# A new hand-written order for the prologue of a block-sparse attention and gated MLP kernel

## The chip, the core and the metric

The kernel runs on one core of a Trainium2 chip. A core has a matrix engine (TensorE, PE in the profile) and three engines that work on whole tiles: VectorE (DVE), ScalarE (ACT) and GpSimd (POOL). SyncE (SP) only issues transfers here. Each engine executes its own queue of instructions in order, and waits on semaphores for what the others make. The metric is the device time of one execution in microseconds (us), and the time given is the median of several.

## The reference

There are 4 batches, 8 heads, 768 positions and 64 elements per head. Every query attends to the keys less than 16 positions away and to 24 summaries, one for each block of 32 positions (the maximum of the block's keys, and the mean of its values). The result goes through a gated MLP with 512 inputs, 1536 hidden columns and 512 outputs. The weights are float64, everything else is float32.

```python
k_sum = k.reshape(B, H, nb, block, D).max(axis=3)
v_sum = v.reshape(B, H, nb, block, D).mean(axis=3)
mask_l = np.abs(pos[:, None] - pos[None, :]) < window
scores_l = np.where(mask_l, scale * q @ k^T, -1e9)
scores_s = scale * q @ k_sum^T + np.log(block)
a = softmax(concat([scores_l, scores_s]))
x = a @ concat([v, v_sum])              # to [3072 tokens, 512]
g = x @ w_gate
out = (g * sigmoid(g) * (x @ w_val)) @ w_out
```

## The kernel before, in words

The 3072 tokens are worked off in six chunks `k` of 512. Attention of a chunk is done for four head pairs `u`, and the MLP of a chunk for twelve slices `j` of 128 hidden columns.

**Products.** Each MLP product is split into a high and a low part of both operands and needs three matmuls. `gate(k,j)` and `val(k,j)` (L654, tiles `g` and `v`) have 4 x 3 matmuls of 128x512, and so has `down(k,j)` (L701, tiles `acc`). With a third number, as in `gate(0,0,2)`, a step does only the three matmuls of one head pair. `silu` (ACT, L660) reads `g` and writes tile `a`, `mul` (DVE, L665) multiplies it by `v`, `ah` (ACT, L189) rounds it and `al` (L185) takes the rest. Two buffers of `a` exist, so `silu(0,j)` must wait until `al` of the slice before the last has read its `a`. `gate` and `val` share two banks of PSUM, so a `val` begins when the `silu` that reads the older bank is done.

**Weights.** A slice of the weights comes as raw float64 (`w_load`, L208, on SP) and is decoded on the chip: `w_abs` (ACT), four DVE steps `w_c1` L222, `w_c2` L226, `w_s1` L234 and `w_s2` L241, then `w_hi` (a rounding copy, L189 on ACT or L191 on DVE), and last `w_lo` (a subtraction with two inputs in SBUF, L185, on DVE as `=d` or on POOL as `=p`). A `gv` slice is 1024 wide and holds gate and value weights, an `o` slice 512 wide.

**Attention of one head pair.** `keys(1,u)` writes the pooled keys into the key windows `kw`: a POOL copy (L191) from `ks`, and where a batch begins also a DVE reduction (L343) that makes the new `ks` and a second POOL copy. There is one buffer of `ks` for each `u`, so the reduction must wait until the first copy has read the old one. Then come `scores` (PE, banks shared with `g`, `v` and `xo`), `ttr` (DVE, L512), `exp`, `rcp`, `nrm` (L555, on POOL, DVE or ACT), two transposes `tr` (PE, `pp`), their copies `pt`, `out` (PE, `xo`), `split` and `rest` (the high and low part of x, `xh` and `xl`). In chunk 0, `sw` and `sp` make the scores, and `out` and `outp` the products with values and pooled values. A number behind an engine letter in `sw`, `tr` or `fv` asks for so many filler matmuls of 128 columns on the zero tile `warm` (L747). They compute nothing.

**Order.** The first part of the program (all of chunk 0's MLP, the attention of chunks 0 and 1 and all weight decoding) is written as a string of 457 steps, `PROLOGUE`. Each step issues its instructions in turn, and a dependency ties every instruction to the one before it on its engine, so the string alone decides the order on each of the five queues:

```python
for name, args, on in read_steps(PROLOGUE):
    step[name](*args)
for x in traced[n_before:]:
    if x.engine in last:
        after(x, last[x.engine])
    last[x.engine] = x
```

The other five sixths of the MLP follow in a loop that the change doesn't touch.

Of the kernel before, what the change touches and what calls it, by code (L numbers as in the profile page):

```python
# [107 lines left out]
kf(2) qf(2) qf(0) sw(0,2)=cc pool(2) sp(0,2) kf(0) ttr0(0,2) pool(0) exp0(0,2) ttr1(0,2) exp1(0,2)
sw(0,0)=yg2 sp(0,0) kq(1) cst() kq(3) ttr0(0,0) pool(1) rcp(0,2) nrm(0,2)=p ttr1(0,0) exp0(0,0) w_load(0,g)
sw(0,1)=yg6 sp(0,1) w_load(1,gv) vr() ve() exp1(0,0) ttr0(0,1) vo() tr0(0,2)=c9 ttr1(0,1) rcp(0,0) w_abs(0,g)  # L110
exp1(0,1) w_c1(0,g) pool(3) exp0(0,1) w_c2(0,g) w_s1(0,g) w_abs(1,gv) rcp(0,1) tr1(0,2)=g sw(0,3)=cy4 sp(0,3)
ttr0(0,3) nrm(0,0)=p tr0(0,0)=c3 ttr1(0,3) exp0(0,3) exp1(0,3) pt0(0,2)=a w_s2(0,g) w_c1(1,gv) w_c2(1,gv)
rcp(0,3) tr1(0,0)=y nrm(0,1)=p tr0(0,1)=y6 w_s1(1,gv) tr1(0,1)=c nrm(0,3)=d w_s2(1,gv) fv()=g pt1(0,2)=a
w_load(0,v) out(0,2)=c pt0(0,0)=a fvc()=a outp(0,2) pt1(0,0)=a out(0,0)=c tr0(0,3)=c pt0(0,1)=a w_load(0,o)
w_abs(0,v) pt1(0,1)=a w_c1(0,v) w_hi(0,g)=a w_c2(0,v) w_abs(0,o) outp(0,0) tr1(0,3)=y w_lo(0,g)=d w_hi(1,gv)=a
w_s1(0,v) w_load(2,gv) w_c1(0,o) w_s2(0,v) w_load(3,gv) w_lo(1,gv)=d w_c2(0,o) out(0,1)=y split(0,0)=a rest(0,0)
w_s1(0,o) pt0(0,3)=a pt1(0,3)=a outp(0,1) w_abs(2,gv) split(0,1)=a w_load(1,o) w_hi(0,v)=a out(0,3)=g outp(0,3)
room(0) rest(0,1) gate(0,0,0) split(0,2)=a gate(0,0,1) rest(0,2) gate(0,0,2) split(0,3)=a rest(0,3) w_c1(2,gv)
w_abs(3,gv) gate(0,0,3) gate(0,1) silu(0,0) w_c1(3,gv) w_c2(2,gv) w_s2(0,o) w_lo(0,v)=p w_s1(2,gv) w_c2(3,gv)
w_s2(2,gv) w_abs(1,o) val(0,0,0) val(0,0,1) silu(0,1) w_hi(0,o)=a val(0,0,2) w_s1(3,gv) w_c1(1,o) val(0,0,3)  # L120
load(1,0) val(0,1) w_hi(2,gv)=a w_lo(2,gv)=d w_load(2,o) w_c2(1,o) mul(0,0) ah(0,0)=a keys(1,0) gate(0,2)
w_abs(2,o) mul(0,1) w_lo(0,o)=d w_s1(1,o) al(0,0)=d ah(0,1)=a w_s2(3,gv) w_load(3,o) w_load(4,gv) silu(0,2)
scores(1,0) down(0,0) val(0,2) w_s2(1,o) w_hi(3,gv)=a al(0,1)=d ttr0(1,0) pool_values(1,0) ttr1(1,0)
w_lo(3,gv)=p w_abs(4,gv) w_abs(3,o) w_c1(4,gv) w_c1(2,o) w_c2(4,gv) gate(0,3) mul(0,2) val(0,3) w_load(5,gv)
w_s1(4,gv) w_c1(3,o) w_s2(4,gv) exp1(1,0) w_hi(1,o)=a w_c2(3,o) w_lo(1,o)=d exp0(1,0) w_hi(4,gv)=a w_s1(3,o)
w_c2(2,o) w_s2(3,o) w_s1(2,o) w_load(7,gv) w_load(6,gv) rcp(1,0) down(0,1) w_lo(4,gv)=d load(1,1) silu(0,3)
w_abs(5,gv) w_hi(3,o)=a w_c1(5,gv) mul(0,3) gate(0,4) val(0,4) ah(0,2)=a w_abs(7,gv) w_c2(5,gv) w_lo(3,o)=d
w_s1(5,gv) w_s2(2,o) nrm(1,0)=a w_hi(2,o)=a w_s2(5,gv) al(0,2)=d w_hi(5,gv)=a tr0(1,0) silu(0,4) w_abs(6,gv)
w_load(4,o) tr1(1,0) pt0(1,0)=a w_abs(4,o) w_lo(2,o)=d pt1(1,0)=a down(0,2) keys(1,1) mul(0,4) w_c1(6,gv)
w_lo(5,gv)=d w_c1(4,o) scores(1,1) ah(0,4)=a w_c2(6,gv) ah(0,3)=a ttr0(1,1) exp0(1,1) ttr1(1,1) al(0,4)=d  # L130
w_load(5,o) load_values(1,0) w_load(7,o) w_load(6,o) w_c1(7,gv) w_s1(6,gv) values(1,0)=a w_load(9,gv) gate(0,5)
al(0,3)=p w_abs(5,o) w_c2(4,o) w_s2(6,gv) w_load(8,gv) w_s1(4,o) val(0,5) w_c2(7,gv) w_hi(6,gv)=a down(0,3)
# [5 lines left out]
w_c1(8,gv) w_lo(5,o)=d w_s2(9,gv) w_hi(9,gv)=a tr0(1,1) down(0,5) mul(0,7) ah(0,7)=a pt0(1,1)=a keys(1,2)
scores(1,2) pool_values(1,2) tr1(1,1) w_lo(9,gv)=d w_s2(6,o) w_abs(8,o) w_s1(7,o) gate(0,9) ttr0(1,2) ttr1(1,2)
pt1(1,1)=a w_c2(8,gv) out(1,1) ah(0,6)=a load(1,3) w_hi(6,o)=a w_lo(6,o)=d exp0(1,2) al(0,6)=p w_s2(7,o)  # L140
w_c1(8,o) exp1(1,2) w_hi(7,o)=a w_s1(8,gv) al(0,7)=d w_s2(8,gv) w_c2(8,o) val(0,9) down(0,6) w_lo(7,o)=d
w_abs(10,gv) w_abs(9,o) w_c1(9,o) w_hi(8,gv)=a w_c1(10,gv) w_lo(8,gv)=d down(0,7) silu(0,9) rcp(1,2) w_c2(10,gv)
w_s1(10,gv) mul(0,9) split(1,1)=a w_s2(10,gv) w_c2(9,o) nrm(1,2)=a gate(0,8) tr0(1,2) w_hi(10,gv)=a keys(1,3)
w_lo(10,gv)=d w_s1(8,o) val(0,8) ah(0,9)=a rest(1,1) room(1) w_load(11,v) w_load(11,g) silu(0,8) mul(0,8)
load_values(1,2) w_load(10,o) w_load(11,o) w_s2(8,o) pt0(1,2)=a al(0,9)=p w_abs(11,v) ah(0,8)=a w_hi(8,o)=a
w_s1(9,o) al(0,8)=d w_lo(8,o)=d gate(0,10) w_c1(11,v) tr1(1,2) pt1(1,2)=a w_c2(11,v) w_s2(9,o) w_s1(11,v)
w_s2(11,v) scores(1,3) ttr0(1,3) values(1,2)=a w_hi(9,o)=a silu(0,10) down(0,8) ttr1(1,3) val(0,10) w_abs(11,g)
w_c1(11,g) w_c2(11,g) w_lo(9,o)=p out(1,2) w_s1(11,g) w_s2(11,g) w_abs(10,o) exp1(1,3) w_hi(11,g)=d w_c1(10,o)
w_hi(11,v)=a down(0,9) w_lo(11,g)=p exp0(1,3) split(1,2)=d mul(0,10) w_lo(11,v)=d w_c2(10,o) rcp(1,3) ah(0,10)=a
rest(1,2) gate(0,11) w_abs(11,o) w_c1(11,o) w_c2(11,o) load_values(1,3) nrm(1,3)=a w_s1(10,o) tr0(1,3)  # L150
pt0(1,3)=a w_s2(10,o) al(0,10)=d w_hi(10,o)=a silu(0,11) pool_values(1,3) val(0,11) tr1(1,3) pt1(1,3)=a
values(1,3)=a w_s1(11,o) w_lo(10,o)=d down(0,10) w_s2(11,o) out(1,3) w_hi(11,o)=d w_lo(11,o)=p mul(0,11)
# [785 lines left out]
```

## Time and profile before

| | |
|---|---|
| time of the kernel, median of 3 runs | 674.9 us (674.82 to 676.22) |
| the profiled execution's own time | 675.49 us |
| its span in the profile | 673.7 us, granted clock 1.00 |
| PE busy | 667.8 us (99%) |
| DVE busy | 340.1 us (50%) |
| ACT busy | 297.4 us (44%) |
| POOL busy | 138.4 us (21%) |

The span is the time between the first and the last instruction of the profiled execution, and 1.8 us of that execution's time lie around it. A start in the trace counts from the start of the span. A duration on DVE or ACT includes an end that the next instruction overlaps: what an instruction costs in a queue that is full is the distance between two starts.

### The profile page before, as it was taken

The page shows a single profiled execution, that of the slowest core. Times are in us where ns is not written, and L with a number is a line of the kernel's source. Part 1 is how long each engine was busy: PE and PEld are TensorE (multiplying, and loading weights), DVE is VectorE, ACT ScalarE, POOL GpSimd, SP SyncE. Part 2 cuts the span into 40 slices and gives each one's busy share as a digit, 9 for nine tenths or more (in the row PEclk, how much of TensorE's full clock was granted, in tenths as well). Part 3 has the DMA queues.
Part 4 walks back from the last instruction along what each step waited for, and adds up shares of the span by engine and source line. Part 5 has one row for each costly group of instructions (what it writes and reads, how often), then busy time and mean ns, then how long its engine had stood idle before and what let it go on. Part 6 is the DMA issues. An engine that isn't in the chain of part 4 may idle for free.

```text
span 673.7 us, 12397 instructions
## 1 busy us (share of the span) xinstructions
PE 667.8 (99%) x4938; PEld 543.6 (81%) x4938; DVE 340.1 (50%) x952; ACT 297.4 (44%) x729; POOL 138.4 (21%) x131
## 2 busy tenths in 40 slices
...
GB/s 333 332 371 359 41 242 172 51 109 145 56 58 0 56 41 126 84 20 80 103 2 167 52 53 82 12 45 61 59 57 58 0 25 0 63 1 0 1 0 64
DMA packets 72059, 60.37 MB, mean 90 GB/s; under 512 B 42144, under 2 KB 60064, under 8 KB 70464
## 3 DMA queue, kind: packets, MB, share of 16 engines
...
## 4 chain that ended last, share of the span: by engine, by line
PE 97%; DVE 2%; DMA 1%; SPq 0%; issue 0%
PE g L654 30%; PE v L654 29%; PE acc L701 29%; PE xo L619 4%; PE sc L454 2%; DMA kq<-in_kF 1%; PE pp L570 1%; DVE p L512 1%; PE sc L465 1%; PE xo L627 1%; DVE ks L343 0%; PE pv L422 0%; PE end L701 0%; PE pp L747 0%; DVE m_g L226 0%
## 5 line engine op out<-in xcount | busy, mean ns | idle before, releaser
L701 PE MATMUL acc<-w_o,ah 128*128 128x512 f32 x572 | 176.2, 389 | 0.0
L654 PE MATMUL g<-xh,w_gv 128*128 128x512 f32 x480 | 159.7, 394 | 0.0
L654 PE MATMUL v<-xh,w_gv 128*128 128x512 f32 x480 | 157.9, 390 | 0.0
L665 DVE TENSOR_TENSOR a<-v,a 128x512 f32<-128x512 f32 x72 | 49.6, 689 | 199.8 <-PE v L654 198.1
L185 POOL TENSOR_TENSOR al<-a,ah 128x512 fp32r<-128x512 f32 x63 | 81.8, 1299 | 328.0 <-ACT ah L189 328.0
L701 PEld LDWEIGHTS acc<-w_o,ah 128*128 128x128 f32 x572 | 107.4, 188 | 22.2
L189 ACT CAST ah<-a 128x512 fp32r<-128x512 f32 x71 | 44.0, 621 | 168.5 <-DVE a L665 168.5
L701 PE MATMUL acc<-w_o,al 128*128 128x512 f32 x286 | 112.0, 392 | 0.0
L654 PEld LDWEIGHTS g<-xh,w_gv 128*128 128x128 f32 x480 | 90.1, 188 | 20.8 <-ACT w_o L189 0.2
L654 PEld LDWEIGHTS v<-xh,w_gv 128*128 128x128 f32 x480 | 90.1, 188 | 18.9
L660 ACT ACTIVATE a<-g 128x512 f32<-128x512 f32 x72 | 43.1, 599 | 134.7 <-PE g L654 131.7
L654 PE MATMUL g<-xl,w_gv 128*128 128x512 f32 x240 | 93.8, 391 | 0.0
L600 DVE STREAM_TRANSPOSE pt_short<-p_short 32x256 f32<-32x256 f32 x192 | 83.8, 436 | 19.8 <-POOL p_short L555 16.9
L654 PE MATMUL v<-xl,w_gv 128*128 128x512 f32 x240 | 93.4, 389 | 0.0
L701 PEld LDWEIGHTS acc<-w_o,al 128*128 128x128 f32 x286 | 53.7, 188 | 11.4 <-DVE al L185 0.2
L654 PEld LDWEIGHTS v<-xl,w_gv 128*128 128x128 f32 x240 | 45.1, 188 | 9.3
L654 PEld LDWEIGHTS g<-xl,w_gv 128*128 128x128 f32 x240 | 45.1, 188 | 8.8
L528 ACT ACTIVATE p_short<-p_short,nm 128x88 f32<-128x88 f32 x128 | 45.3, 356 | 0.2
L185 DVE TENSOR_TENSOR xl<-xo,xh 128x512 fp32r<-128x512 f32 x24 | 16.4, 686 | 57.0 <-ACT xh L189 56.9
L555 POOL TENSOR_TENSOR p_short<-p_short,ri 128x704 f32<-128x704 f32 x16 | 26.0, 1623 | 53.5 <-DVE ri L546 49.6
L654 PE MATMUL g<-xh,w_g 128*128 128x512 f32 x96 | 32.2, 396 | 0.0
L654 PE MATMUL v<-xh,w_v 128*128 128x512 f32 x96 | 31.6, 390 | 0.0
...
## 6 DMA issues: line engine op xcount, KB each, us to landing
raw_gv<-in_wgv SPq DMA_DIRECT2D x10, 1024.0 KB, 11.9
...
```

What stands on the lines that cost most here:

```text
L185: (nc.vector if e == "d" else nc.gpsimd).tensor_tensor(out=out, in0=a, in1=b.bitcast(F32), op=ALU.subtract)
L189: nc.scalar.copy(out, in_)
L454: nc.tensor.matmul(sc[h][s * SQ : (s + 1) * SQ, c * SC : (c + 1) * SC], t["q"][hs, i * SQ : (i + 1) * SQ], keys[hs], start=True, stop=True,)
L465: nc.tensor.matmul(sc[h][s * QT : (s + 1) * QT, c * KC : (c + 1) * KC], t["q"][hs, qs], t["kw"][hs, i, :], start=True, stop=True,)
L528: nc.scalar.activation(out=t["p"][:, i, :kc], in_=t["p"][:, i, :kc], func=AF.Exp, scale=-1.0, bias=t["nm"][:, i : i + 1], accum_out=t["sm" ...
L555: (nc.vector if on == "d" else nc.gpsimd).tensor_tensor(out=p, in0=p, in1=ri.rearrange("p (n o) -> p n o", o=1).broadcast_to([P, 2 * NTP, ...
L600: nc.vector.transpose(out=to[r * SQ : (r + 1) * SQ, :, s * SQ : (s + 1) * SQ], in_=t["p"][s * SQ : (s + 1) * SQ, :, at : at + SQ],)
L619: nc.tensor.matmul(ps[hs, qs], vw, t["pt"][:n, h, qs], start=k not in OWN or i == 0, stop=k not in OWN)
L654: nc.tensor.matmul(ps, w[:, cs], x, start=u == 0 and n == 0, stop=u == NP - 1 and n == 2)
L660: nc.scalar.activation(out=a, in_=A.pop(("g", k, j)), func=AF.Silu)
L665: nc.vector.tensor_tensor(out=a, in0=ps, in1=a, op=ALU.mult)
L701: nc.tensor.matmul(out, a[:, ts], w[:, cs], start=begin and n == 0, stop=end and n == 2)
```

## The change

The string is replaced by another order of the 457 steps. Some steps also get another engine: of the `w_lo`, 13 are on POOL instead of 6, five of them 1024 wide (slices 1, 3, 7, 9, 10) where there was one; of chunk 0's `al`, two are on POOL instead of four; `nrm(0,1)` goes from POOL to DVE. Chunk 0's first products are interleaved by head pair (`gate(0,0,0) gate(0,0,2) val(0,0,0) gate(0,0,1) ...`), with `w_v0` ready early, where all of gate slices 0 and 1 stood ahead of value slice 0. The fillers go from 37 units of 128 columns to 16 (of both, 7 are the opening ones). Two functions are adapted: slice 11's lead is on the other half, and `a_max` allocates its tiles in whichever half comes first. Line numbers from `a_max` on grow by one.

```diff
@@ PROLOGUE, the steps around keys(1,2), of 52 lines that are all new
-w_abs(7,o) w_abs(9,gv) w_c1(9,gv) w_c1(7,o) val(0,6) w_hi(7,gv)=a w_lo(7,gv)=d w_c2(9,gv) split(1,0)=a w_s2(5,o)
...
+rcp(1,1) silu(0,6) w_c1(6,o) w_c2(6,o) nrm(1,1)=a w_lo(7,gv)=p w_abs(8,gv) val(0,6) w_lo(4,o)=d keys(1,2)
...
     def w_lead(j, nm):
-        return LEAD if (nm, j) == ("v", NJ - 1) else 0
+        return LEAD if (nm, j) == ("g", NJ - 1) else 0
...
         t = U[k, u]
-        if g == 0 and k >= SHORT:
+        first = "p" not in t
+        if first and k >= SHORT:
             t["p"] = short["p"]
-        elif g == 0:
+        elif first:
...
-        if g == 0:
+        if first:
```

In the rows below a name is a tile with its slice or chunk and head pair, and a running number at its end; `w_gv7_1161<-m_gv7_1007` is a subtraction that makes the low half of weight slice 7.

POOL's queue from the first `w_lo` to the copies for the scores of chunk 1, head pair 2, before:

```order
L185 TENSOR_TENSOR w_v0_567<-m_v0_505,w_v0_567 128x512
L191 COPY kw_1_0_668<-ks_0_161 128x4x24
L191 COPY kw_1_0_668<-ks_0_696 128x4x24
L185 TENSOR_TENSOR w_gv3_776<-m_gv3_615,w_gv3_776 128x1024
L191 COPY kw_1_1_876<-ks_1_224 128x4x24
L191 COPY kw_1_1_876<-ks_1_973 128x4x24
L185 TENSOR_TENSOR al_0_3_1052<-a_0_3_881,ah_0_3_1001 128x512
L185 TENSOR_TENSOR w_o4_1128<-m_o4_956,w_o4_1128 128x512
L185 TENSOR_TENSOR al_0_5_1213<-a_0_5_1106,ah_0_5_1206 128x512
L191 COPY kw_1_2_1196<-ks_2_134 128x4x24
L191 COPY kw_1_2_1196<-ks_2_1286 128x4x24
```

The same stretch of POOL's queue, and one row more, of the change:

```order
L185 TENSOR_TENSOR w_gv1_568<-m_gv1_322,w_gv1_568 128x1024
L185 TENSOR_TENSOR w_o1_754<-m_o1_648,w_o1_754 128x512
L191 COPY kw_1_0_694<-ks_0_183 128x4x24
L191 COPY kw_1_0_694<-ks_0_775 128x4x24
L185 TENSOR_TENSOR w_gv3_835<-m_gv3_711,w_gv3_835 128x1024
L191 COPY kw_1_1_909<-ks_1_246 128x4x24
L191 COPY kw_1_1_909<-ks_1_1000 128x4x24
L185 TENSOR_TENSOR w_o2_1009<-m_o2_838,w_o2_1009 128x512
L185 TENSOR_TENSOR w_o3_1003<-m_o3_667,w_o3_1003 128x512
L185 TENSOR_TENSOR w_gv7_1161<-m_gv7_1007,w_gv7_1161 128x1024
L191 COPY kw_1_2_1054<-ks_2_134 128x4x24
L191 COPY kw_1_2_1054<-ks_2_1195 128x4x24
```

The subtractions of weight slices 1, 7 and 9 (the last in the next row) are now POOL's, `al_0_5` is no longer, and the copies of each head pair stand behind a subtraction of weights.

DVE's queue at the reduction for `keys(1,2)` before, where `ks_2_1286` is the new pooled keys:

```order
L185 TENSOR_TENSOR w_o5_1203<-m_o5_1054,w_o5_1203 128x512
L241 SCALAR_TENSOR_TENSOR m_gv9_1158<-raw_gv9_1037,m_gv9_1158 128x1024
L665 TENSOR_TENSOR a_0_7_1233<-v_0_7_1245,a_0_7_1233 128x512
L343 TENSOR_REDUCE ks_2_1286<-kt_1_2_1191 128x24
L363 TENSOR_REDUCE vr_1_2_1307<-vt_1_2_1199 128x24
L185 TENSOR_TENSOR w_gv9_1261<-m_gv9_1158,w_gv9_1261 128x1024
```

The same place in DVE's queue of the change:

```order
L185 TENSOR_TENSOR w_o4_1154<-m_o4_699,w_o4_1154 128x512
L343 TENSOR_REDUCE ks_2_1195<-kt_1_2_1049 128x24
L185 TENSOR_TENSOR xl_1_0_1127<-xo_1_0_1059,xh_1_0_1126 128x512
L666 TENSOR_TENSOR a_0_6_1165<-v_0_6_1180,a_0_6_1165 128x512
L234 SCALAR_TENSOR_TENSOR m_gv9_960<-raw_gv9_778,m_gv9_960 128x1024
L222 TENSOR_SCALAR m_o5_1093<-m_o5_1093 128x512
L226 TENSOR_SCALAR m_o5_1093<-m_o5_1093 128x512
L234 SCALAR_TENSOR_TENSOR m_o5_1093<-raw_o5_855,m_o5_1093 128x512
L234 SCALAR_TENSOR_TENSOR m_o6_1148<-raw_o6_1011,m_o6_1148 128x512
L241 SCALAR_TENSOR_TENSOR m_o5_1093<-raw_o5_855,m_o5_1093 128x512
L241 SCALAR_TENSOR_TENSOR m_gv9_960<-raw_gv9_778,m_gv9_960 128x1024
L185 TENSOR_TENSOR al_0_5_1253<-a_0_5_983,ah_0_5_1158 128x512
```

The reduction has moved ahead of `xl_1_0` and `mul(0,6)` (tile `a_0_6`), and `al_0_5` has come to DVE, eleven rows behind it.

## Rows read from the trace of the kernel before

**Rows 1.** The longest wait of PE behind the opening: us in total, times, longest.
```profile
PE sc L479 <- DMA kq<-in_kF: 0.9, 1, 0.9
```

**Rows 2.** Stretch, us, busy (count): PE, PEld, DVE, ACT, POOL; clock, DMA share, GB/s.
```profile
10.00:20.00 10.00, 9.66 (x159) 6.49 (x158) 9.86 (x58) 10.00 (x48) 5.44 (x3) 1.00 1.02 402
30.00:140.00 110.00, 110.00 (x718) 88.78 (x715) 108.12 (x221) 95.25 (x201) 18.91 (x20) 1.00 0.57 193
```

**Rows 3.** Timeline of PE up to the first gate product: start, duration, what.
```profile
1.46 3.35 PE L747 MATMUL warm<-warm 128*128 128x512 f32 x4 [1.46 <-DVE warm L809]
...
12.29 2.21 PE L747 MATMUL pp<-warm 128*128 128x512 f32 x6
...
23.68 1.15 PE L619 MATMUL xo<-pt,vrows 96*64 96x64 f32 x32
...
32.53 0.50 PE L654 MATMUL g<-xh,w_g 128*128 128x512 f32 x1
```

**Rows 4.** Timeline of SP: the last transfer that the `out` products need.
```profile
7.95 0.33 SPq L791 DMA_DIRECT2D vrows<-in_vO  x1
```

**Rows 5.** Transfers: queue, count, size, median us from issue to landing.
```profile
vrows<-in_vO SPq DMA_DIRECT2D x1, 1024.0 KB, 15.3
```

**Rows 6.** Timeline of POOL: start, duration, what, idle time before and its releaser.
```profile
14.61 1.85 POOL L555 TENSOR_TENSOR p<-p,ri 128x960 f32<-128x960 f32 x1 [0.88 <-DVE ri L546]
...
48.82 2.42 POOL L185 TENSOR_TENSOR w_gv<-m_gv,w_gv 128x1024 fp32r<-128x1024 f32 x1 [4.37 <-ACT w_gv L189]
...
91.23 1.29 POOL L185 TENSOR_TENSOR al<-a,ah 128x512 fp32r<-128x512 f32 x1 [8.53 <-ACT ah L189]
...
97.34 0.27 POOL L191 COPY kw<-ks 128x96 f32<-128x96 f32 x1 [4.41 <-DVE ks L343]
```

**Rows 7.** Timeline of DVE, 15 to 50 us.
```profile
15.59 1.15 DVE L226 TENSOR_SCALAR m_g<-m_g 128x512 int32<-128x512 int32 x1
...
22.96 1.15 DVE L555 TENSOR_TENSOR p<-p,ri 128x960 f32<-128x960 f32 x1
...
32.42 2.01 DVE L185 TENSOR_TENSOR xl<-xo,xh 128x512 fp32r<-128x512 f32 x3
...
37.90 0.68 DVE L226 TENSOR_SCALAR m_gv<-m_gv 128x1024 int32<-128x1024 int32 x1
38.50 1.22 DVE L241 SCALAR_TENSOR_TENSOR m_gv<-raw_gv,m_gv 128x1024 int32<-128x1024 int32 x1
...
42.24 0.42 DVE L226 TENSOR_SCALAR m_o<-m_o 128x512 int32<-128x512 int32 x1
42.57 0.68 DVE L665 TENSOR_TENSOR a<-v,a 128x512 f32<-128x512 f32 x1
43.17 0.94 DVE L343 TENSOR_REDUCE ks<-kt 128x24 f32<-128x768 f32 x1
44.03 0.68 DVE L665 TENSOR_TENSOR a<-v,a 128x512 f32<-128x512 f32 x1
```

**Rows 8.** Timeline of ACT, 28 to 41 us.
```profile
28.94 0.63 ACT L189 CAST xh<-xo 128x512 fp32r<-128x512 f32 x1
29.41 1.12 ACT L189 COPY pt<-pp 120x512 f32<-120x512 f32 x2
...
38.32 0.60 ACT L660 ACTIVATE a<-g 128x512 f32<-128x512 f32 x1 [1.20 <-PE g L654]
...
39.80 1.05 ACT L189 CAST w_gv<-m_gv 128x1024 fp32r<-128x1024 f32 x1 [0.37 <-DVE m_gv L241]
```

**Rows 9.** The chain that ended last, 88 to 106 us: start, length, what.
```profile
92.16 2.72 PE v L654 x12
94.89 0.44 PE pp L570 x4
...
98.07 0.98 PE sc L465 x32
...
102.39 1.08 PE xo L619 x32
```

More of the change, by code (lines that the diff above doesn't have):

```diff
@@ L107 @@
 PROLOGUE = """
[L108 to L132, printed above, removed]
@@ L138 @@
[L138 to L152, printed above, removed]
@@ new lines @@
+w_hi(0,g)=a w_s1(2,gv) split(0,0)=a w_hi(1,gv)=a outp(0,1) w_load(3,o) w_load(1,o) w_load(2,o) split(0,2)=a
+w_lo(0,g)=d split(0,1)=a outp(0,3) rest(0,0) rest(0,2) split(0,3)=a gate(0,0,0) rest(0,1) gate(0,0,2) rest(0,3)
+val(0,0,0) w_abs(0,o) w_c1(0,o) gate(0,0,1) w_abs(4,gv) gate(0,0,3) val(0,0,2) w_c2(0,o) silu(0,0) w_s1(0,o)
+w_c1(4,gv) w_load(5,gv) val(0,0,1) w_load(3,gv) room(0) w_s2(0,o) w_s2(2,gv) w_lo(1,gv)=p w_hi(2,gv)=a
+w_hi(0,o)=a val(0,0,3) w_abs(1,o) w_c2(4,gv) mul(0,0) gate(0,1) w_lo(2,gv)=d w_lo(0,o)=d w_abs(3,o) ah(0,0)=a
```

45 lines of the change are left out of this document (40 added, 5 removed).

## The prediction

> **What bounds the kernel now.** I first asked what the matrix engine waits for. The span holds two short stages. In the first, up to the first gate product at 32.53 us [rows 3], PE is not the limit. It has one wait of 0.9 us there [rows 1] and fills the other gaps with products on the zero tile (six of them, 2.21 us, at 12.29 [rows 3]). The transfers are the limit: between 10 and 20 us the DMA engines are fully busy at 402 GB/s [rows 2]. The last transfer that the `out` products need, `vO`, is issued at 7.95 [rows 4] and takes 15.3 us [rows 5], so it lands at 23.2. The first `out` starts at 23.68, and from there PE works without a gap to the gate at 32.53 (8.85 us) [rows 3].
>
> From the gate on PE itself is the limit. Between 30 and 140 us it is busy for 110.0 of 110 us, but DVE is close behind it with 108.1, while POOL has 18.9 [rows 2]. So PE's time is safe only as long as DVE's queue, or what DVE waits for, is not late. Here the reader should look: there is hardly any room on DVE, and any wait in its queue comes out on PE a little later.
>
> **The prices.** In a full DVE queue an instruction costs its duration less the 0.08 that the next one overlaps [rows 7]: two inputs of 1024 columns 1.14, two inputs of 512 columns 0.60, one input of 1024 columns 0.60, one input of 512 columns 0.34, the reduction 0.86; and 0.12 more for a decoding step with one input right behind the step that it reads (an estimate from the gaps of this kind). A subtraction of weights of 1024 columns costs POOL 2.42, one of 512 columns 1.29, a copy into `kw` 0.27 [rows 6]. On ACT, `silu` is 0.60 and a rounding copy of 1024 columns 1.05 [rows 8]. On PE a group of twelve matmuls is 2.72, scores 0.98, four transposes 0.44, `out` 1.08 [rows 9].
>
> **One price decides.** DVE and POOL hinder each other on SBUF. POOL's `nrm` runs from 14.61 to 16.46 [rows 6]. DVE's `w_c2` starts inside it at 15.59 and takes 1.15 [rows 7] where another of its size takes 0.42 [rows 7]: it ends 0.28 after POOL does. So I count a DVE instruction with two SBUF inputs, or one of the fast one-input ones, as held until POOL's subtraction ends, and POOL's likewise. The change puts seven more `w_lo` on POOL, at twice DVE's price (2.42 against 1.14).
>
> The Trainium skill (SBUF — State Buffer, "SBUF: two separate sides") says the same more strictly: the pair of ports that GpSimd and VectorE share is an exclusive lock, held for the whole instruction by whichever started first. The row of 1.15 agrees. By that rule, moving subtractions to POOL frees DVE of nothing while POOL's run overlaps such DVE work; its sum is the forecast's; by the opposite reading DVE would gain 1.14 for each, and the sum would be that of the second rival. The sum below goes by the rows alone.
>
> **Before the gate: nothing, at best.** `vO` stands behind the same bytes in both orders (`raw_v0` went ahead of it and `raw_g0` behind it, both 512 KB), so it lands at 23.2 again, and four `out`, four `outp` and two pairs of transposes still lie behind it. The fillers that go (21 units) lay in gaps that the transfers make, and leave idle time. On DVE the new order has `nrm(0,1)` more (1.07; POOL had it) before `nrm(0,3)`, which was at 22.96 [rows 7] and comes to about 24.1. Behind it stand two inputs of 1024, 960 and five of 512 columns with the one-input steps of `g0` and `gv2`: 1.07 + 1.14 + 0.46 + 0.46 + 0.72 + 0.60 + 0.72 + 0.72 + 1.14 = 7.0, so `w_lo(0,g)` starts at 31.1, and with its 0.60 and `xl_0_0`'s 0.68 x is ready at 32.4. PE arrives at 32.5. I take 0. From below the bound is -0.5 (23.68 less 23.2); the upper one is the first rival.
>
> **The scores of chunk 1, pair 0: +0.8.** The last `xl` ends at 34.4 now (32.42 + 2.01 [rows 7]) and at about 34.1 in the new order. From there DVE has 22 instructions to the end of `w_lo(4,gv)`: six of two inputs and 1024 columns (6.84), seven of two and 512 (4.20), five of one and 1024 (3.00), four of one and 512 (1.36), five pauses (0.60): 16.0, to 50.1. POOL's `w_lo(1,o)`, ready during the last, is held until its end: 1.29, then the copy 0.27, on which DVE's reduction waits (0.86), then the second copy 0.27, with 0.2 for four hand-overs: 2.9, so the scores can start at 53.0. PE has seven groups of 2.72 from 32.53, and about 0.6 for changes of tile: 52.2. In the old order there were five groups, and no wait.
>
> **The scores of pair 2: +3.3.** DVE stays full from 34.1 to `w_lo(4,o)`, 102 instructions: 15 of two inputs and 1024 columns (17.1), 24 of two and 512 (14.4), 12 of one and 1024 (7.2), 13 of one and 512 (4.4), four reductions (3.4), 16 steps of maxima at 0.20 (3.3) and two `rcp` (0.6), 50.4 in all; with the wait above (0.9) and pauses (1.3) it gets to 86.7. PE has 18 groups (49.0), two scores (2.0), two pairs of transposes (1.0), `out` (1.1), 0.8 of waiting and some 0.4 of changes, and begins `down(0,4)` at 86.8. So both arrive there together, and about then, at 86.6, POOL starts `w_lo(7,gv)`.
>
> Now the chain. POOL takes 2.42 and the copy 0.27: 89.3. DVE waits for that copy with its reduction (2.7 us idle, with `xl_1_0` and `mul(0,6)` behind it). Then 0.86 + 0.60 + 0.60 + 1.14 + 0.46 + 0.46 + 0.60 + 0.60 + 0.60 + 1.14 + 0.69 = 7.75 to the end of `al(0,5)`: 97.1. This subtraction frees the `a` into which `silu(0,7)` writes (0.60), and `silu` frees the bank for `val(0,7)`: 97.8. PE reaches that point after 2.72 + 0.44 + 2.72 + 0.44 + 0.98 + 1.08 = 8.4 at 95.2, so it loses 2.5 in two places: about 0.9 at pair 1's transposes and pooled values, whose `nrm` and bank come late too, and 1.6 at `val(0,7)`. Behind `silu` ACT rounds slice 9 (1.05), POOL, after some 0.3 of DVE work that holds it, subtracts it (2.42): 101.5. PE ends `val(0,7)` at 100.6 and loses 0.9 more. Sum 3.3. In the old order none of this stands in line: `al(0,5)` is POOL's at 91.23, and the reduction is just ahead of POOL's copy at 97.34 [rows 6], with `w_lo(7,gv)` long done on DVE.
>
> **Behind it: +0.3** (from -0.5 to +1.0). Five more POOL subtractions stand in front of gate 10, gate 11 and the last `down`; four small waits there, of 0.1 to 0.35, are set off by fewer changes between kinds of PE work.
>
> The sum is 0 + 0.8 + 3.3 + 0.3 = +4.4 on a span of 673.7. The profiled execution took 675.49, 0.6 above the median; I add the 4.4 to the median: **679.3 us**. A change under 0.2% (1.35 us) can't be told from none.
>
> **Rivals.** *POOL comes first at 31.1.* `w_lo(1,gv)` on POOL waits for ACT's rounding of slice 1. ACT's queue from the landing of `raw_gv2` (three transfers' bytes after `vO`, 1.5 MB at 402 GB/s: 27.0) is `w_abs` 1.03, two `pt` (0.96), two copies of 512 (1.06) and one of 1024 (1.05): 31.1, the very time of DVE's `w_lo(0,g)`. If POOL is first, DVE is held for 2.42: the gate comes 2.3 later, and the time is 681.6. Against it only that the sums are equal. 0.32.
>
> *They hinder each other less than I count.* Then `w_lo(1,o)` needn't wait for `w_lo(4,gv)` (the 0.8 goes), and the chain at pair 2 keeps only the waits by semaphore, 1.6 less: 674.9 + 2.0 - 0.8 = 676.1 or, with PE's fewer changes, about 675.6. Against it stands the row of 1.15. 0.12.
>
> *Faster.* The first gate is set by the landing of `vO`, and 0.5 lies between it and the first `out`; DMA share 1.02 leaves nothing before it. If `vO` landed 1.0 us earlier through the other order of transfers, and the chain at pair 2 fitted (`al(0,5)` done by 94.5, 2.6 earlier than I add), it would be 673.4. It decides from a landing before 22.4. 0.07.
>
> *The clock.* The four opening fillers took 0.84 us each, at the lower level of 1.2 GHz, the six at 12.29 0.37 each, at 2.4 GHz [rows 3]. The idle gaps that the removed fillers leave, of up to 1.7 us before 21 us, could bring the lower level back; the granted clock is 1.00 throughout now, also around the wait of 0.9. Half speed for the two microseconds of products on the way to the gate costs 2: 681.3. 0.05.
>
> **How the numbers follow.** My forecast has 0.44, and its own range is 677.8 to 680.6. With POOL first (0.32) and the clock (0.05) most lies between 677.8 and 682.3; the milder case (0.12) reaches down to 675.6. The range is 675.6 to 682.4, which leaves out the faster case and the outer ends. Slower by over 0.2%: forecast, POOL first, clock, and a little of the milder case, 0.82; within: most of the milder case, 0.11; faster: 0.07.
>
> **What would show it.** Right: DVE idle for about 2.7 at L343 between 80 and 92 us, released by POOL's copy; PE waiting 1 to 2 us before a `v` near 98 for ACT's `silu`, and under 1 before a `g` near 102 for POOL's `w_gv`; a wait before scores near 53 for POOL's `kw`; the first gate at 32.5 (or 34.8 in the first rival). Wrong: the first gate before 32, a DVE instruction that runs unhindered inside a POOL subtraction, or a PE without waits from 85 to 103.

## The result and the profile after

The changed kernel takes 681.8 us, median of 6 runs (679.7 to 683.1), against 675.0 of the kernel before, median of 6 runs beside it (674.8 to 676.2). The ratio is 1.0094, 95% interval 1.0075 to 1.0113: slower by 6.3 us (5.1 to 7.6). The sign was forecast, and the time lies in the range given, near its upper end; the forecast of 4.4 us more was too low.

The profiled execution took 680.39 us, 1.4 below the median, with a span of 678.6: 4.9 more than before. PE is busy for 667.0 us of it (before 667.8), with fewer fillers and some work at a lower clock, so it stands idle for 5.7 us more. Here are the waits of PE that answer to [rows 1], of 0.3 us and more (engine, tile and line, what was waited for; us in total, times, longest):

```profile
PE sc L491 <- DVE ks L343: 2.0, 1, 2.0
PE sc L479 <- DMA kq<-in_kF: 1.7, 1, 1.7
...
PE v L655 <- ACT a L661: 1.1, 1, 1.1
PE sc L479 <- DMA kq<-in_kq: 0.8, 1, 0.8
PE g L655 <- POOL w_gv L185: 0.6, 1, 0.6
PE sc L465 <- POOL kw L191: 0.4, 1, 0.4
PE g L655 <- ACT a L661: 0.3, 1, 0.3
```

Before, one wait of scores stood in the head; now there are three (2.0, 1.7 and 0.8). Further down stand the three that the prediction named: `kw` (pair 0), `a` from ACT (slice 7) and `w_gv` from POOL (slice 9). The timeline of PE, against [rows 3], says when:

```profile
8.48 0.89 PE L479 MATMUL sc<-kq 64*64 64x96 f32 x32 [1.73 <-DMA kq<-in_kF]
...
19.06 0.66 PE L491 MATMUL sc<-ks,kq 64*64 64x24 f32 x32 [2.02 <-DVE ks L343]
19.66 3.53 PE L571 MATMUL pp<-consts,p 128*120 128x128 f32 x16
...
25.98 2.09 PE L620 MATMUL xo<-pt,vrows 96*64 96x64 f32 x64
...
32.65 1.89 PE L628 MATMUL xo<-pt,vs 120*64 120x512 f32 x8
34.55 0.50 PE L655 MATMUL g<-xh,w_g 128*128 128x512 f32 x1
...
55.01 0.64 PE L465 MATMUL sc<-kw,q 64*64 64x120 f32 x16 [0.42 <-POOL kw L191]
...
98.81 0.50 PE L655 MATMUL v<-xh,w_gv 128*128 128x512 f32 x1 [1.09 <-ACT a L661]
...
102.44 0.50 PE L655 MATMUL g<-xh,w_gv 128*128 128x512 f32 x1 [0.62 <-POOL w_gv L185]
```

The first gate product starts at 34.55 where it started at 32.53. So of the 4.9 us of span 2.0 come before the gate, for which the sum had nothing, and 2.9 behind it, for which the sum had 4.4. In this execution PE comes to the gate without a wait: its last `outp` products end at 34.54 (32.65 + 1.89). The windows (columns as in [rows 2]) show PE no longer full behind the gate, and two stretches of the head at the lower level of 1.2 GHz:

```profile
10.00:13.00 3.00, 2.94 (x48) 1.94 (x44) 2.77 (x20) 2.58 (x14) 0.00 (x0) 0.50 1.01 412
...
20.00:23.00 3.00, 3.00 (x15) 2.77 (x13) 2.93 (x20) 2.95 (x15) 1.35 (x2) 0.50 0.99 406
...
30.00:140.00 110.00, 107.57 (x730) 86.33 (x727) 102.86 (x215) 90.09 (x194) 28.59 (x21) 1.00 0.56 191
```

The last row answers to the second of [rows 2]: PE has 2.4 us less, POOL 9.7 more, and DVE 5.3 less: it was relieved of subtractions, and for 7.1 us (110 less 102.86) it stands idle. Where it waits, its timeline shows, against [rows 7]:

```profile
8.37 0.95 DVE L343 TENSOR_REDUCE ks<-kq 128x24 f32<-128x768 f32 x1 [0.52 <-DMA kq<-in_kF]
...
16.64 1.32 DVE L546 TENSOR_SCALAR sm<-sm 128x8 f32<-128x8 f32 x1
...
25.96 1.16 DVE L556 TENSOR_TENSOR p<-p,ri 128x960 f32<-128x960 f32 x1
...
33.21 0.68 DVE L185 TENSOR_TENSOR w_g<-m_g,w_g 128x512 fp32r<-128x512 f32 x1
33.81 2.48 DVE L185 TENSOR_TENSOR xl<-xo,xh 128x512 fp32r<-128x512 f32 x4
...
53.68 0.95 DVE L343 TENSOR_REDUCE ks<-kt 128x24 f32<-128x768 f32 x1 [0.78 <-POOL kw L191]
...
90.38 0.95 DVE L343 TENSOR_REDUCE ks<-kt 128x24 f32<-128x768 f32 x1 [2.50 <-POOL kw L191]
...
97.44 0.68 DVE L185 TENSOR_TENSOR al<-a,ah 128x512 fp32r<-128x512 f32 x1
```

And POOL's, against [rows 6]:

```profile
16.14 1.79 POOL L556 TENSOR_TENSOR p<-p,ri 128x960 f32<-128x960 f32 x1 [12.82 <-DVE nm L513]
...
33.55 2.60 POOL L185 TENSOR_TENSOR w_gv<-m_gv,w_gv 128x1024 fp32r<-128x1024 f32 x1 [12.20 <-ACT w_gv L189]
51.30 2.14 POOL L185 TENSOR_TENSOR w_o<-m_o,w_o 128x512 fp32r<-128x512 f32 x1 [15.14 <-ACT w_o L189]
...
87.37 2.77 POOL L185 TENSOR_TENSOR w_gv<-m_gv,w_gv 128x1024 fp32r<-128x1024 f32 x1 [8.90 <-ACT w_gv L189]
90.08 0.26 POOL L191 COPY kw<-ks 128x96 f32<-128x96 f32 x1
```

Read DVE's reduction at 90.38 beside the last two rows of POOL: the subtraction of slice 7, the copy into `kw` behind it, and 2.50 us in which DVE stands before its reduction (2.7 forecast). `al(0,5)` follows at 97.44, and PE's `v` at 98.81, released by ACT's `silu`. The chain is the one that the prediction wrote down, at times 0.8 to 1.0 later.

`vO` lands no later than it did: it is issued at 8.36 (before 7.95, [rows 4]) and takes 14.3 (before 15.3, [rows 5]), which makes 22.7 instead of 23.2. But PE's first `out` starts at 25.98 instead of 23.68 [rows 3]: PE waits 2.02 for a reduction of DVE, and the 16 transposes behind it take 3.53 at the lower level, where they take 1.97 in a variant below whose clock is 1.00 (the one with the later rounding).

### The profile page after: what moved, and what is told of

Read it like the earlier page. It is cut to its first block, busy times and chain, and to the rows that moved or that the text cites. A ratio compares the mean times of both kernels' runs of the same rounds, so it can differ in the third digit from the quotient of the medians.

```text
span 678.6 us, 12374 instructions
## 1 busy us (share of the span) xinstructions
PE 667.0 (98%) x4924; PEld 544.6 (80%) x4924; DVE 341.2 (50%) x955; ACT 290.9 (43%) x720; POOL 149.0 (22%) x135
## 4 chain that ended last, share of the span: by engine, by line
PE 83%; issue 6%; DMA 6%; ACT 1%; POOL 1%; DVE 1%; SPq 0%; POOLq 0%
PE acc L702 26%; PE g L655 26%; PE v L655 25%; DMA raw_gv<-in_wgv 6%; PE xo L620 3%; PE sc L454 2%; POOL w_o L185 1%; ACT p L529 0%; POOL w_gv L185 0%; DVE m_gv L234 0%; ACT p L554 0%; PE end L702 0%; DVE w_o L185 0%; POOL kw L191 0%; PE pp L571 0%
## 5 line engine op out<-in xcount | busy, mean ns | idle before, releaser
L185 POOL TENSOR_TENSOR al<-a,ah 128x512 fp32r<-128x512 f32 x61 | 78.8, 1291 | 309.0 <-ACT ah L189 309.0
L655 PE MATMUL g<-xh,w_g 128*128 128x512 f32 x96 | 32.5, 398 | 0.3 <-ACT a L661 0.3
```

The lines of the kernel that those rows point to most:

```text
L185: (nc.vector if e == "d" else nc.gpsimd).tensor_tensor(out=out, in0=a, in1=b.bitcast(F32), op=ALU.subtract)
L655: nc.tensor.matmul(ps, w[:, cs], x, start=u == 0 and n == 0, stop=u == NP - 1 and n == 2)
```

## The experiments

Two accounts were set against each other: that DVE and POOL take turns on SBUF, so that subtractions moved to POOL give DVE nothing and put POOL's work in line; and that the loss comes from something else, above all the clock, since the change took 21 units of fillers away. Each expectation names its own two. The kernel before took between 674.9 and 675.5 us (medians) on these chips.

**Fillers and clock.** The kernel before without its fillers, the seven opening ones excepted:

```diff
-sw(0,0)=yg2 ... sw(0,1)=yg6 ... tr0(0,2)=c9 ... sw(0,3)=cy4 ... tr0(0,0)=c3 ... tr0(0,1)=y6
+sw(0,0)=yg  ... sw(0,1)=yg  ... tr0(0,2)=c  ... sw(0,3)=cy  ... tr0(0,0)=c  ... tr0(0,1)=y
```

> The kernel before without its 30 units of filler products ahead of the first gate (the opening 7 stay). Theory 1 (fillers keep the clock up): granted clock falls to half between 9 and 23 us, the first gate comes 1 to 2.5 us later, time 676 to 677.5. Rival (fillers only fill idle time, and the transfers set the gate): the first gate within 0.3 of 32.5 and the time within 0.2% of before.

Measured: 674.8 us (674.4 to 676.2), ratio 0.9997 (0.9988 to 1.0006), no change. A window, a wait and the first gate of its profile:

```profile
16.00:20.00 4.00, 2.94 (x72) 2.66 (x72) 3.93 (x21) 4.00 (x18) 2.46 (x2) 0.82 1.00 405
```

```profile
PE xo L619 <- DMA vrows<-in_vO: 0.4, 1, 0.4
```

```profile
32.43 0.50 PE L654 MATMUL g<-xh,w_g 128*128 128x512 f32 x1
```

The clock does fall (0.82 in this window), and it costs nothing: the `out` products wait for `vO`, which the fillers had covered, and the gate starts when it did. In the old order the fillers only fill time.

The other way round, the change with fillers put back (a new step `fill` puts eight of them ahead of `sp(0,3)`):

```diff
-sw(0,0)=gc ... sw(0,3)=gc7  ... w_abs(1,gv) sp(0,3)
+sw(0,0)=gc6 ... sw(0,3)=gc10 ... w_abs(1,gv) fill(0,0,1)=c8 sp(0,3)
```

> The changed order with filler products put into PE's three idle gaps before the first gate (6 units of 128 columns ahead of the near scores of pair 0, 10 instead of 7 ahead of those of pair 3, 8 behind them), so that the clock should not fall. Theory 1 (the first gate is 2.0 us late because PE runs at the lower level from 9.8 to 13 and from 20 to 23 us): granted clock 1.00 throughout, the first gate at 32.6 to 33.2, time 1.4 to 2.0 below the changed kernel, near 679.5 to 680. Rival (the first gate is late because VectorE's queue is full from 8.4 to 34.4 us and does not shorten): clock 1.00, but the first gate stays at 34.2 to 34.6 and the time falls by less than 0.5.

Measured: 684.2 us (683.1 to 685.5), ratio 1.0137 (1.0123 to 1.0151), 2.4 slower than the change. Rows of POOL, DVE and PE around the gate, and a window:

```profile
33.21 2.58 POOL L185 TENSOR_TENSOR w_gv<-m_gv,w_gv 128x1024 fp32r<-128x1024 f32 x1 [12.11 <-ACT w_gv L189]
...
33.51 2.84 DVE L185 TENSOR_TENSOR w_g<-m_g,w_g 128x512 fp32r<-128x512 f32 x1
...
37.00 0.50 PE L660 MATMUL g<-xh,w_g 128*128 128x512 f32 x1 [2.79 <-DVE xl L185]
```

```profile
38.00:41.00 3.00, 3.00 (x9) 2.28 (x8) 2.93 (x7) 0.82 (x1) 0.00 (x0) 0.52 1.00 415
```

Neither account had this. The clock was 1.00 up to the gate, but POOL's subtraction of slice 1 came 0.30 us ahead of DVE's `w_lo(0,g)`, which then took 2.84 instead of 0.68. PE waited 2.79, and behind the wait came 3 us at the lower level (0.52), with eight matmuls some 0.2 longer each, 1.6 in all. This is the prediction's first rival. The fillers had also made DVE wait for scores once more (0.72), and `w_lo(0,g)` started no earlier for them. In the profile of the change itself DVE wins by 0.34 (33.21 against 33.55).

**The chain at pair 2.** Slices 7 and 9 back to DVE, `al(0,5)` to POOL, as before the change:

```diff
-w_lo(7,gv)=p ... al(0,5)=d ... w_lo(9,gv)=p
+w_lo(7,gv)=d ... al(0,5)=p ... w_lo(9,gv)=d
```

> The changed order with the subtractions of weight slices 7 and 9 back on VectorE and al(0,5) back on POOL, all else as changed. Theory 1 (the stall around 90 to 102 us is POOL's 2.4 us each, and VectorE's wait for POOL's copy behind it): no wait of VectorE at the reduction for pair 2, no waits before the value product of slice 7 and the gate product of slice 9 (1.1 and 0.6), the span from the first gate to the end 1.7 to 2.4 shorter. Rival (VectorE is full anyway, so 2.3 us of subtractions more on it come out at PE): that span changes by less than 0.5.

Measured: 682.7 us (682.2 to 683.4), ratio 1.0115 (1.0101 to 1.0129). DVE's wait at the reduction and PE's waits at slices 7 and 9 are gone, and one at the gate stands in the list instead:

```profile
PE g L655 <- DVE xl L185: 2.8, 1, 2.8
```

POOL had won again (32.72 against 33.02), and the gate came at 36.51. So the waits are shown to come from these three engine letters. The time isn't: from the first gate to the end of the span it is 644.5 us here and 644.1 in the change, where 1.7 to 2.4 less was expected, and by the expectation's own measure the rival came. The lower level followed the wait here too (0.56 from 38 to 41); in the kernel with fillers that cost about 1.6, and here it may have hidden a gain, which isn't shown.

The same chain cut elsewhere, with the copy ahead of the subtraction:

```diff
-nrm(1,1)=a w_lo(7,gv)=p w_abs(8,gv) val(0,6) w_lo(4,o)=d keys(1,2)
+nrm(1,1)=a keys(1,2) w_lo(7,gv)=p w_abs(8,gv) val(0,6) w_lo(4,o)=d
```

> The changed order with one step moved: keys of chunk 1, pair 2, ahead of POOL's subtraction of weight slice 7, which stays on POOL, as do all others. Theory 1 (what costs is the wait by semaphore: POOL's copy queued behind a 2.4 us subtraction, and 2.5 us of VectorE behind the copy): VectorE's wait goes, the waits at 98.8 and 102.4 fall by 1.2 to 1.7 in sum, time from the first gate 1.2 to 1.9 shorter. Rival (the two engines' hindering on SBUF costs it): waits fall by less than 0.5.

Measured: 682.1 us (681.3 to 683.7), ratio 1.0108 (1.0095 to 1.0122). The wait of slice 7 is gone, that of slice 9 stays (0.6), and PE waits 0.5 for a `w_o` of DVE that is late in its place. From the first gate to the end it takes 643.5 us, 0.6 less than the change, where 1.2 to 1.9 was expected. In this profile the gate starts at 36.02, late for another reason, which a window shows:

```profile
20.00:25.00 5.00, 5.00 (x56) 4.53 (x56) 4.50 (x23) 4.20 (x19) 1.59 (x2) 0.50 1.01 412
```

PE worked at 1.2 GHz for five microseconds of the way to the gate, DVE waited for scores twice (0.68 and 0.38) and once for ACT (0.91), and reached `w_lo(0,g)` at 34.69. As in the change, PE came to the gate without a wait.

**The race at the gate.** ACT's rounding of slice 1, which releases POOL, moved behind two steps:

```diff
-w_hi(0,g)=a w_s1(2,gv) split(0,0)=a w_hi(1,gv)=a outp(0,1) ... split(0,2)=a w_lo(0,g)=d split(0,1)=a outp(0,3)
+w_hi(0,g)=a w_s1(2,gv) split(0,0)=a outp(0,1) ... split(0,2)=a w_lo(0,g)=d split(0,1)=a w_hi(1,gv)=a outp(0,3)
```

> The changed order with one ScalarE step moved: the rounding of weight slice 1 behind the x copies of pairs 2 and 1, so that POOL's subtraction of it gets ready about 1.0 us later (33.7 instead of 32.7) and comes after VectorE's subtraction of gate slice 0 (33.0). Theory 1 (whichever of the two starts first holds SBUF; in the profiles of the two variants where POOL was first by 0.3 us, VectorE's subtraction took 2.8 instead of 0.7, PE waited 2.8 at the gate and then ran at the lower level for 3 us): no wait of PE for xl at the first gate beyond 0.8, the first gate at 34.2 to 34.8, granted clock 1.00 between 38 and 41, time near 679.5 to 680.5. Rival (the 2.8 comes from something else that is late on VectorE): the first gate stays at 36 to 37.

And the subtraction of slice 1 on DVE instead:

```diff
-w_s2(0,o) w_s2(2,gv) w_lo(1,gv)=p w_hi(2,gv)=a
+w_s2(0,o) w_s2(2,gv) w_lo(1,gv)=d w_hi(2,gv)=a
```

> The changed order with the subtraction of weight slice 1 on VectorE instead of POOL, where the text has it, behind the four xl. Theory 1 (the same): POOL holds nothing there, the first gate at 34.2 to 34.8, no wait of PE for xl beyond 0.8, and VectorE is 1.1 us later behind it, so the scores of pair 0 wait 1.0 to 1.5 instead of 0.4; time 680 to 681. Rival (the race decides nothing): as the changed kernel, 681.8, with the first gate at 36 to 37.

Measured: 680.8 us (five runs from 680.2 to 681.2, one of 685.2), ratio 1.0097 (1.0078 to 1.0116), and 681.4 us (680.9 to 682.1), ratio 1.0097 (1.0084 to 1.0110): neither can be told from the change. The rows of the first, DVE, POOL and PE:

```profile
32.52 0.68 DVE L185 TENSOR_TENSOR w_g<-m_g,w_g 128x512 fp32r<-128x512 f32 x1
33.12 2.48 DVE L185 TENSOR_TENSOR xl<-xo,xh 128x512 fp32r<-128x512 f32 x4
35.51 1.21 DVE L222 TENSOR_SCALAR m_o<-m_o 128x512 f32<-128x512 f32 x1
...
34.02 2.42 POOL L185 TENSOR_TENSOR w_gv<-m_gv,w_gv 128x1024 fp32r<-128x1024 f32 x1 [13.16 <-ACT w_gv L189]
...
33.86 0.50 PE L655 MATMUL g<-xh,w_g 128*128 128x512 f32 x1 [0.64 <-DVE xl L185]
...
55.69 0.50 PE L655 MATMUL g<-xh,w_gv 128*128 128x512 f32 x1
```

The race is out of the way, the clock is 1.00 from start to end, and the gate comes at 33.86, waiting for DVE. It is still 1.3 later than before, and without that wait PE would have begun it at 33.22. (In the second kernel `w_lo(0,g)` starts at 32.52 and the gate at 33.86 as well.) The last row says why 0.7 gained at the gate is worth nothing: the gate product behind pair 0's scores starts at 55.69, in the change at 55.59. DVE and POOL set that place, and DVE lost what it had gained: POOL's later subtraction now holds its step at 35.51 (1.21, in the change 0.42). The second kernel missed its expectation: PE waits 0.3 at pair 0's scores, not 1.0 to 1.5, and 1.1 for DVE's slice 1 instead.

**The head.** In the next kernel POOL takes `nrm(0,1)` back, three decoding steps of slice 2 go behind the first gate products, and slice 1 is DVE's:

```diff
-nrm(0,1)=d ... w_s1(0,g) w_s2(0,g) w_c1(2,gv) w_c2(2,gv) w_hi(0,g)=a w_s1(2,gv) ... rest(0,3) ... w_lo(1,gv)=p
+nrm(0,1)=p ... w_s1(0,g) w_s2(0,g) w_hi(0,g)=a ... rest(0,3) w_c1(2,gv) w_c2(2,gv) w_s1(2,gv) ... w_lo(1,gv)=d
```

> The changed order with VectorE's queue ahead of the first gate made shorter: nrm(0,1) back on POOL (1.07 less), the first three decoding steps of weight slice 2 behind the last xl (2.6 less), and slice 1's subtraction on VectorE. Theory 1 (VectorE's queue, full from 8.4 us on, makes the first gate late): w_lo(0,g) at 29.5 to 30.5, no wait of PE for xl, the first gate at 32.5 to 33.5, set by the transfers and PE again, time 677 to 679, with what stays lost behind the gate. Rival (PE's lower clock and its late products ahead of the gate are the cause): the first gate at 34 or later in the profile, and a time that scatters as before by 3 us.

And the same with slices 7 and 9 and `al(0,5)` put back as above:

> The kernel of the run before it, and besides the subtractions of weight slices 7 and 9 on VectorE and al(0,5) on POOL. Theory 1 (what is lost behind the gate is the chain at pair 2, with PE's waits of 1.1 and 0.6 and the products behind them): 1.3 to 2.4 less than that kernel, 675.2 to 677. Rival (VectorE's queue is as late without it): within 0.7 of that kernel.

Measured: 685.0 us (683.8 to 686.4), ratio 1.0150 (1.0137 to 1.0163), and 683.8 us (683.3 to 684.3), ratio 1.0129 (1.0115 to 1.0144). Both are slower than the change. POOL and DVE in the first:

```profile
22.55 2.06 POOL L556 TENSOR_TENSOR p<-p,ri 128x960 f32<-128x960 f32 x1 [1.84 <-DVE ri L547]
24.58 1.71 POOL L185 TENSOR_TENSOR w_v<-m_v,w_v 128x512 fp32r<-128x512 f32 x1
...
23.00 2.16 DVE L226 TENSOR_SCALAR m_gv<-m_gv 128x1024 int32<-128x1024 int32 x1
25.20 2.18 DVE L234 SCALAR_TENSOR_TENSOR m_gv<-raw_gv,m_gv 128x1024 int32<-128x1024 int32 x1
```

DVE saved 1.07 by giving `nrm(0,1)` away and was held 1.5 us by it and 1.0 by the subtraction behind it (2.16 and 2.18, where the same two take 0.69 and 1.23 in the change). `w_lo(0,g)` came at 33.02, not at 29.5 to 30.5, and the gate at 35.42. In the second kernel, whose clock is 1.00 up to the gate, they came at 31.76 and 34.16. Of the two signs that the expectation named, that of the rival came, a gate at 34 or later: PE reached it without a wait in both, after waiting 0.7 for POOL's `nrm` and 1.2 for DVE's. So PE's late products count at the gate beside DVE's queue, and they need no lower clock for it. The steps moved behind the gate came back as a wait of 3.4 us of PE for `w_gv`. Taking the chain at pair 2 out is worth 1.2 here (1.3 to 2.4 expected).

A smaller edit, on top of the later rounding of slice 1: `rcp(0,2)` ahead of `rcp(0,0)`, so that no tiny step of DVE meets the first `nrm` of POOL:

```diff
-rcp(0,0) ttr1(0,1) rcp(0,2) pool(3)
+rcp(0,2) rcp(0,0) ttr1(0,1) pool(3)
```

> The variant with the rounding of slice 1 later, and besides rcp(0,2) ahead of rcp(0,0), so that both stand on VectorE before POOL's nrm(0,0) begins (a tiny VectorE step of rcp(0,2) is held 1.14 us by it in the changed kernel). Theory 1 (VectorE's queue is full from 8.4 to about 100 us and carries every delay on to PE): every VectorE step behind it about 1.1 earlier, the first gate at 32.5 to 33.0, PE at the scores of pair 2 and at the end 0.8 to 1.2 earlier, time 679.6 to 680.0 against 680.8 without. Rival (what is gained at the gate is lost again behind it, as when the gate came 0.7 earlier and the scores of pair 0 no earlier): time within 0.3 of 680.8.

Measured: 680.5 us (679.8 to 681.7), ratio 1.0072 (1.0059 to 1.0085). Rows of DVE and POOL:

```profile
15.95 0.12 DVE L546 TENSOR_SCALAR sm<-sm 128x8 f32<-128x8 f32 x1
...
20.59 0.69 DVE L546 TENSOR_SCALAR sm<-sm 128x8 f32<-128x8 f32 x1
...
16.49 3.54 POOL L556 TENSOR_TENSOR p<-p,ri 128x960 f32<-128x960 f32 x2 [13.17 <-DVE nm L513]
19.98 1.28 POOL L185 TENSOR_TENSOR w_v<-m_v,w_v 128x512 fp32r<-128x512 f32 x1
```

The hold of 1.32 is gone, and POOL's next subtraction holds the next tiny step (0.69); DVE also waits 0.40 and 0.23 for scores of PE, and `nrm(0,3)` comes at 25.66, no earlier than without the edit (25.46). The gate comes at 34.05, the rival's result: part of the hold had moved, and part became waits.

**All known waits out.** On top of that, pair 0's copy ahead of the subtractions, and in a second kernel slices 7 and 9 and `al(0,5)` put back too:

```diff
-w_lo(4,gv)=d w_hi(1,o)=a down(0,0) mul(0,1) w_lo(1,o)=p keys(1,0)
+keys(1,0) w_lo(4,gv)=d w_hi(1,o)=a down(0,0) mul(0,1) w_lo(1,o)=p
```

> The kernel of the run before it, and besides the keys of pair 0 ahead of VectorE's subtraction of slice 4 and POOL's of output slice 1, so that the scores of pair 0 need not wait for these. Theory 1: the wait there (0.4 to 0.7) goes; VectorE has as much to do until pair 2, so there the waits grow by as much, and the time is within 0.4 of the kernel before. Rival (each wait costs by itself): 0.4 to 0.8 less.

> The kernel of the run before it, and besides slices 7 and 9 subtracted on VectorE and al(0,5) on POOL. Theory 1 (with the chain at pair 2 gone as well, hardly a wait is left behind the gate): 1.0 to 2.0 less than the kernel before it, 677.5 to 678.8, and what remains over 674.9 is the later first gate and waits of 0.3 to 0.5 at single products. Rival (VectorE's queue is the limit as a whole): less than 0.7.

Measured: 680.4 us (679.3 to 680.8), ratio 1.0065 (1.0053 to 1.0078), and 680.0 us (679.5 to 681.0), ratio 1.0069 (1.0055 to 1.0082). In the first the wait of pair 0's scores is gone, in the second those of slices 7 and 9 too, and in its list stands this:

```profile
PE g L655 <- DVE w_gv L185: 1.4, 3, 0.8
```

Of the second kernel's 3.9 us of span above the kernel before, 1.2 come before the gate (33.72) and 1.7 stand in the list of waits behind it (this row, and 0.3 for ACT's `a`). The second was expected to take 1.0 to 2.0 less than the first and takes 0.3 less: the rival's result, in which DVE's queue as a whole is the limit.

**The price of POOL by itself.** The kernel before, with nothing but the engine of three subtractions changed:

```diff
-w_lo(1,gv)=d ... w_lo(7,gv)=d ... w_lo(9,gv)=d
+w_lo(1,gv)=p ... w_lo(7,gv)=p ... w_lo(9,gv)=p
```

> The kernel before, in its own order, with the subtractions of weight slices 1, 7 and 9 on POOL (three of the five that the change puts there). Theory 1 (POOL's subtraction is twice as long and VectorE's instructions with two inputs in SBUF wait for it, so nothing is gained): slice 1's run from 29.1 to 31.5 holds VectorE by over 1.5, the first gate comes 0.5 to 1.5 later, time 675.5 to 677.5. Rival (VectorE gains 1.14 for each): 674.9 or less, with VectorE idle more.

Measured: 678.6 us (678.4 to 679.0), ratio 1.0042 (1.0030 to 1.0055): slower by 2.8 us (2.0 to 3.7), with the clock at 1.00, and more than expected (675.5 to 677.5). POOL, DVE and PE around its gate:

```profile
28.94 2.89 POOL L185 TENSOR_TENSOR w_gv<-m_gv,w_gv 128x1024 fp32r<-128x1024 f32 x1 [9.38 <-ACT w_gv L189]
...
29.51 2.60 DVE L226 TENSOR_SCALAR m_o<-m_o 128x512 int32<-128x512 int32 x1
...
32.63 1.68 DVE L234 SCALAR_TENSOR_TENSOR m_o<-raw_o,m_o 128x512 int32<-128x512 int32 x1
...
34.97 0.50 PE L654 MATMUL g<-xl,w_g 128*128 128x512 f32 x1 [1.24 <-DVE xl L185]
```

A decoding step of 0.42 [rows 7] took 2.60 and ended 0.28 after POOL did. The first gate product isn't late (32.31); PE waits 1.24 behind it for the next `xl` (last row), and 0.6 in all for slices 7 and 9: 1.8 of the 2.9 us of span. Over the first 105 us DVE is busy for 97.29 us here and for 96.90 in the kernel before, although three subtractions of 1.14 left its queue: what it gave away it got back, as far as the rows show, as time held. This is the cleanest run of the study, since order, fillers and clock are those of the kernel before. Three engine letters cost nearly half of what the whole change costs.

None of the kernels beats the kernel before; the one without fillers equals it.

## Why the prediction was right in sign and short in size

**The price that decides** was right. For the DVE instructions that the prediction counted, DVE and POOL exclude each other on SBUF, and the kernel with three letters changed puts a number on it. The rule that the prediction cited from the Trainium skill (SBUF — State Buffer, "SBUF: two separate sides"), a lock for the whole instruction by whichever came first, agrees with 2.60 for 0.42 above. Not every DVE instruction is held: the four `xl`, with one input in PSUM, run at 0.60 each inside POOL's subtraction (33.81, 2.48 against 33.55, 2.60). By its words the prediction's sign of being wrong, a DVE instruction that runs unhindered there, came; but `xl` isn't of the kind that its sum counts as held.

**The scores of pair 0** were right: 0.8 forecast; PE waits 0.4, and from the first scores at 53.95 to the next gate product at 55.59 it takes 1.64 where scores cost 0.98, so it loses 0.7. Moving the copy took the wait away.

**The scores of pair 2** were right in the chain and too large in sum: 2.50 of DVE's wait against 2.7; 1.1 at `val(0,7)` against 1.6; 0.6 at gate 9 against 0.9; nothing at pair 1's transposes and pooled values against 0.9. That last term was the mistake: PE passes them at 91.75 and 95.05 without a wait. The late gate made the other waits smaller, since POOL and DVE set the time of this place: gate 9 was forecast at 101.5 and came at 102.44, only 0.9 later than forecast, and a PE that is late anyway waits less for it. With the gate 0.7 earlier, in the variant with the later rounding, gate 9 came at 102.58.

**Behind it** +0.3: of about the right size; PE waits 0.3 for ACT's `a`.

**Before the gate: nothing, at best** is the step that failed. It let DVE start `w_lo(0,g)` at 31.1, from a `nrm(0,3)` at 24.1. `nrm(0,3)` came at 25.96. The difference can be read: the prediction counted `nrm(0,1)` (1.07) but not the tiny step of 128x8, which POOL's `nrm` holds from 16.64 on (1.32 against 0.17, 1.15 more), nor the cast of `w_v`, which takes 0.34 of DVE's queue at 15.21. That makes 24.03 + 1.15 + 0.34 = 25.5, close to where it stands (25.46) in the kernel with the later rounding, whose clock is 1.00. The sum closes better than it should: the old 22.96 contains holds that the new order is rid of (1.15 for 0.42 at 15.59 [rows 7], 0.7), and waits and pauses of the new order make up for them. In the change itself 0.5 comes on top: `kF` releases the first reduction at 8.37 instead of about 8.1, and DVE waits 0.23 for PE. From `nrm(0,3)` to `w_lo(0,g)` it took 7.25, and the sum had 7.0. So the prediction's rule was right, and it wasn't applied far enough up the queue: I considered what POOL's `w_lo` would hold, and the transfer that had set the gate, while DVE's queue had taken over from the transfer. The other half of the step, that PE arrives at 32.5, failed as well: it arrives at 34.54 in the profiled execution and at 33.22 in the kernel with the later rounding, because its products stand behind DVE's reduction and, in the former, run at the lower clock. At 34.5 DVE's first `xl` and PE's last product end together (33.81 + 0.68 and 34.54), so each alone would have set this gate.

**The sum** came near the span (4.4 against 4.9) through two misses of opposite sign, 2.0 too little before the gate and 1.5 too much behind it. That is in part luck, and in part the place at pair 2, which takes in what is late before it.

**The rival that POOL comes first** (0.32): POOL came second in the profiled execution by 0.34 us and first in two of its variants, where it costs 2.16 on DVE (2.84 less 0.68), a wait of 2.8 on PE and a gate 2.0 and 2.4 later than the change's (2.3 forecast). The median of 681.8 is nearly this rival's 681.6; which of the two came first in the executions that make it isn't on record, so that proves nothing. **The clock** (0.05) has a share that I gave too little weight. Without fillers the old order loses nothing, because a transfer sets its gate. In the new order DVE's queue and PE's own products set it, DVE waits for scores that PE makes at 1.2 GHz, and the gates of the profiled executions with a low clock between 20 and 25 us were at 34.55 and 36.02, against 33.72 to 34.05 at 1.00 in the four whose head is the change's but for one or two moved steps, and in which POOL doesn't come first (with a smaller dip, 0.83 between 20 and 23, the kernel with pair 0's copy moved had its gate at 33.49). But the clock isn't the whole: three variants whose profiled execution had it at 1.00 throughout took 680.5, 681.1 and 681.7 us in it. What the low clock follows can be read too: in the five profiles of changed kernels where PE had waited 1.6 to 2.4 us for the transfer `kF` around 8 us, the granted clock from 10 to 13 us was 0.50 to 0.69; in all the others, where that wait was 1.0 or less, it was 1.00. Between the change and the kernel with the later rounding the order up to there is the same, and the wait was 1.7 and 0.9, so it differs from execution to execution. **Milder hindering** and **faster** are out.

**What stays open.** Of the 2.5 us by which the forecast is low, 0.5 stand in the profile (4.9 against 4.4), 0.6 come from adding to the median what was worked out on an execution 0.6 above it, and 1.4 are the distance of the change's profiled execution from its median. Its runs spread over 3.5 us. Both the race and the clock can make such steps, but only one execution was profiled, so their shares in the median aren't shown. The granted clock over the whole span is on record for all six: the four at 0.992 took 681.7 to 683.1, those at 0.995 and 0.997 took 680.4 and 679.7; in the variant with the later rounding three at 1.00 took 680.2 to 680.6. In the last of the kernels with all known waits out, 1.0 of 3.9 us of span isn't assigned. That DVE's queue as a whole is what keeps the new order slow fits the small gain of each edit, but no run isolates it.
